# Attention and gated FFN in one kernel: another tile for unread products, a margin in the planner, new ranks

## The chip, the cores and the metric

The kernel runs on one core of one Trainium2 chip. The core has a matrix engine (TensorE, PE in the profile; its weight loads are listed as PEld), VectorE (DVE), ScalarE (ACT), GpSimd (POOL), the queue engine SyncE (SP), and 16 DMA engines. Each engine works through its own list of instructions in order. The metric is the time of one execution on the device in microseconds (us), lower is better.

## The reference

Eight batches, eight heads, 576 tokens, head size 64, and 16 extra "beacon" keys and values in front that every query sees. Causal attention over 592 keys, then a gated FFN over all 4608 tokens (512 to 1536 to 512):

```
scores = scale * q @ [beacon_k, k].T          # per batch and head
scores = where(causal, -1e9, scores)
a      = exp(scores - max) / (sum + 1e-9)
x      = a @ [beacon_v, v]                    # heads side by side: 4608 x 512
out    = (relu(x @ w_gate) * (x @ w_val)) @ w_out
```

Inputs and output are float32.

## The kernel before, in words

**Tiling.** All products are bfloat16 with float32 sums in PSUM, which has eight banks of 128 x 512. Heads go in pairs `p` (four per batch `b`). For a batch the keys and queries are loaded by `load_pair` into staging tiles `st`, cast to bfloat16 (`rounded`, tile `h`, line 487), turned by a product with the identity `ident` (`turned`, line 498), and copied out of PSUM into `kT` and, for queries, into a block-diagonal tile `diag` that holds both heads of a pair (lines 439 and 441 are the helper `copy`). `load_rest` does the same for the first tokens with the beacon keys ("F" in the order strings) and for the last ones ("L"). `load_v` loads and casts values (line 443).

**Attention.** A batch's queries are cut into blocks named A, B, C, D, E, with 128 of diag's rows for two heads at a time, and a last block F of 16 tokens that takes all heads together. `tile_step` issues the score products (line 670; 662 and 665 for E and F), the row minimum with the mask on VectorE (lines 682 and 685), the exponential on ScalarE (696), the reciprocal of the sums on VectorE (708, 703 adds two sums) and the normalization on GpSimd (715). In batch 0 the normalized blocks are turned by TensorE (line 750); in later batches by a DMA transpose on SP's queue (line 761). Then come the value products (771; 800 for F), and copies into `xT`.

**FFN.** `hidden` (lines 838, 842, 846) makes the gate and value products for 512 tokens of a batch, in the first three batches cut at token 240, with relu on ScalarE and the product on VectorE into `hT`. `project` (858) multiplies by `wo_r` in three parts of four products, copies and stores (870). The last 64 tokens of each batch are gathered for four batches at a time. The first part of the FFN of batch 0 needs the AB blocks of all four pairs and the first weights.

**The order.** Nothing is scheduled by hand. Each step is a `Task` with an engine, a cost, dependencies, buffers and a rank; `Plan.order` (line 162) simulates the engines with these costs and writes the tasks out in the order in which it starts them. Among tasks that could start at the same time the lower rank goes first. Every engine's list is fixed by this. The constants at the top (RANK, AHEAD, STEPS, ORDER0 and so on) are ranks and thresholds of that planner. STEPS gives the ranks of the groups of blocks for batches 0 to 2, WHOLE for the later ones. W_FROM and W_STEP give the earliest planned issue of the nine weight loads, which GpSimd issues (line 456) between its other work; loads of batch 1 and on wait for the first of them (`gated`).

**Unread products.** Where the planner sees TensorE idle in the first 100 us, it inserts `Filler`s: products of 256 columns (`fill`, line 917) into a bank that nobody reads. Before, they read `ident` and `mask`, two tiles that GpSimd writes (lines 379 to 387). Up to 6 us they are counted at 0.97 of the gap and a spacing of 0.2137 us, rounded down, later at 0.75 of the gap and 0.107 us.

## Time and profile before

| | us |
|---|---|
| median of 3 runs | 413.88 |
| lowest and highest | 412.75, 414.21 |
| the profiled execution's own time | 413.18 |
| its span, first to last instruction | 411.4 |
| TensorE busy | 396.4 |
| VectorE, ScalarE, GpSimd busy | 320.4, 287.0, 233.7 |

A row of the timeline reads: start, duration, engine, line, operation, output<-input, shape, count, and in brackets the idle time of the engine before it and what ended it. A row of a table of stretches reads: stretch, its length, busy time and count of PE, PEld, DVE, ACT and POOL, clock, DMA share, GB/s. A row of waits reads: who waited for whom, total, times, longest. Matmuls are pipelined: the duration of one includes its way through the array, so the spacing of the starts tells the pace.

### The profile page before, as it was taken

The numbers are of one execution on the slowest core, as the hardware profiler recorded it, in microseconds if no ns is written. First come the engines' busy times: TensorE is split into PE (matmuls) and PEld (weight loads), VectorE is DVE, ScalarE is ACT, GpSimd is POOL, SyncE is SP. The second block draws the span as 40 slices with busy tenths as digits, with TensorE's granted clock in tenths as the row PEclk, the third lists the DMA queues.
The fourth block names the chain that finished last, engine by engine and source line by source line (L and its number), as shares of the span: only waits on it lengthen the run. The fifth ranks groups of instructions, "written<-read, shape, count | busy, mean of one in ns | idle before, by whom it ended". The sixth has DMA issues, their size and how long they took to land.

```text
span 411.4 us, 10350 instructions
## 1 busy us (share of the span) xinstructions
PE 396.4 (96%) x3278; PEld 249.2 (61%) x3315; DVE 320.4 (78%) x1163; ACT 287.0 (70%) x956; POOL 233.7 (57%) x433
## 2 busy tenths in 40 slices
PE   7899999999999999999999989999999999999994
PEld 4667878487856877545558654554555545444483
DVE  6899989898989889889789898997895844233251
ACT  5898999786979899797669787874884853033040
POOL 5799769657695688568748874982761620000000
PEclk9999999999999999999999999999999999999999
DMA  8899969999999999998989699969809872110112
GB/s 199 163 236 225 211 158 174 185 186 249 177 200 184 221 229 207 200 244 151 216 216 248 192 216 170 242 153 221 158 2 209 152 105 57 57 47 0 53 53 52
DMA packets 172616, 68.03 MB, mean 165 GB/s; under 512 B 146832, under 2 KB 168080, under 8 KB 172560
## 3 DMA queue, kind: packets, MB, share of 16 engines
q1 hardware_dynamic: 167808, 62.64, 74.1%
q0 software_dynamic: 4752, 4.72, 7.0%
q8 instruction: 26, 0.43, 0.4%
q14 instruction: 30, 0.25, 0.2%
HBM read 38.27 MB, written 9.44 MB: 116 GB/s over the span
## 4 chain that ended last, share of the span: by engine, by line
PE 60%; DVE 3%; issue 2%; POOL 1%; ACT 1%; DMA 1%; SPq 0%; POOLq 0%; ACTq 0%; DVEq 0%
PE f L838 32%; PE f L858 17%; PE f L670 4%; PE f L771 4%; PE f L498 2%; PE f L662 1%; DMA st<-in_beacon_v_dram 1%; ACT pb L696 1%; POOL pb L715 1%; DVE f L685 1%; PE f L800 1%; DVE diag L441 1%; DVE osb L441 0%; DVE small L703 0%; POOL h L487 0%
## 5 line engine op out<-in xcount | busy, mean ns | idle before, releaser
L715 POOL TENSOR_SCALAR pb<-pb,small 128x576 bf16<-128x576 bf16 (+8 forms) x224 | 122.3, 564 | 76.1 <-DVE small L708 63.8
L696 ACT ACTIVATE pb<-f,small 128x64 bf16<-128x64 f32 (+6 forms) x256 | 131.6, 528 | 17.8 <-DVE small L685 9.5
L685 DVE CUSTOM_DVE_ANT_0 f<-f,mask 128x448 f32<-128x448 f32 (+7 forms) x256 | 111.7, 474 | 6.5 <-PE f L670 5.0
L842 ACT ACTIVATE g<-f 128x512 f32<-128x512 f32 (+3 forms) x156 | 71.4, 471 | 64.5 <-PE f L838 57.4
L838 PE MATMUL f<-xT,wv_r 128*128 128x512 bf16 (+3 forms) x617 | 110.6, 313 | 0.8 <-ACT pb L696 0.4
L838 PE MATMUL f<-xT,wg_r 128*128 128x512 bf16 (+3 forms) x615 | 109.4, 312 | 0.5
L846 DVE TENSOR_TENSOR hT<-g,f 128x512 bf16<-128x512 f32 (+3 forms) x156 | 79.8, 519 | 32.0 <-PE f L838 29.2
L858 PE MATMUL f<-wo_r,hT 128*128 128x512 bf16 (+1 forms) x426 | 100.7, 373 | 0.9
L838 PEld LDWEIGHTS <-wv_r 128*128 128x128 bf16 x624 | 59.0, 98 | 33.7 <-issue 0.8
L838 PEld LDWEIGHTS <-wg_r 128*128 128x128 bf16 x624 | 59.8, 98 | 31.8
L858 PEld LDWEIGHTS <-hT 128*128 128x128 bf16 x444 | 41.6, 98 | 40.4 <-issue 0.2
L696 ACT ACTIVATION_READ_ACCUMULATOR pb<-f,small 128x1 f32 x256 | 55.0, 215 | 0.0
L670 PE MATMUL f<-kT,diag 128*128 128x128 bf16 (+4 forms) x255 | 46.0, 286 | 0.8 <-DVE hT L846 0.7
L685 DVE DVE_READ_ACCUMULATOR2_ANT small<- 128x1 f32 x296 | 40.8, 138 | 0.2
L487 POOL TENSOR_SCALAR h<-st 128x512 bf16<-128x512 f32 x62 | 38.0, 620 | 4.7 <-DMA st<-in_q_dram 2.7
L441 DVE COPY osb<-f 128x512 f32<-128x512 f32 (+1 forms) x27 | 18.3, 680 | 24.0 <-PE f L858 23.7
L441 DVE CAST diag<-f 64x512 bf16<-64x512 f32 (+2 forms) x52 | 28.5, 553 | 5.0 <-PE f L498 2.7
L498 PE MATMUL f<-ident,h 128*128 128x128 bf16 (+2 forms) x320 | 29.3, 220 | 3.2 <-POOL h L487 1.5
L498 PEld LDWEIGHTS <-h 128*128 128x128 bf16 (+2 forms) x320 | 21.5, 99 | 15.1 <-POOL h L487 4.4
L715 POOL TENSOR_SCALAR xT<-xT,small 128x64 bf16<-128x64 bf16 (+4 forms) x64 | 27.4, 444 | 5.0 <-DVE small L708 4.5
L682 DVE TENSOR_REDUCE small<-f 128x1 f32<-128x512 f32 x40 | 27.3, 682 | 3.0 <-PE f L662 2.2
L696 ACT ACTIVATE xT<-f,small 128x64 bf16<-128x64 f32 (+3 forms) x64 | 27.6, 446 | 2.4 <-DVE small L685 1.7
(68 smaller groups left out, 371.9 us busy)
## 6 DMA issues: line engine op xcount, KB each, us to landing
st<-in_k_dram SPq DMA_DIRECT2D x32, 256.0 KB, 4.4
st<-in_q_dram SPq DMA_DIRECT2D x32, 256.0 KB, 4.1
out_dram<-osb SPq DMA_DIRECT2D x32, 256.0 KB, 2.8
st<-in_v_dram SPq DMA_DIRECT2D x24, 256.0 KB, 5.1
st<-in_v_dram SPq DMA_DIRECT2D x8, 224.0 KB, 4.6
wg_r<-in_moe_w_gate_dram POOLq DMA_DIRECT2D x3, 512.0 KB, 7.9
wv_r<-in_moe_w_val_dram POOLq DMA_DIRECT2D x3, 512.0 KB, 10.1
wo_r<-in_moe_w_out_dram POOLq DMA_DIRECT2D x3, 512.0 KB, 14.3
```

What stands on the lines that cost most here:

```text
L441: nc.vector.tensor_copy(dst, src)
L487: (nc.gpsimd if x.engine == "POOL" else nc.vector).tensor_scalar(to, of, by, 1.0, ALU.mult, ALU.mult)
L498: nc.tensor.matmul(to, h16.tile[:rows, a * P:(a + 1) * P], ident[:rows, :rows], start=True, stop=True)
L670: nc.tensor.matmul(view(i), t.diag.tile[:, p, j * P:j * P + P], kT[:, p, :n], start=True, stop=True)
L682: nc.vector.tensor_reduce(out=to, in_=view(i), axis=AX.X, op=ALU.min)
L685: nc.vector.tensor_tensor_reduce(out=view(i), in0=view(i), in1=msk, scale=1.0, scalar=small["t"][:, 0:1] if name in "EF" else 3.0e38, op0= ...
L696: nc.scalar.activation(ph.tile.rearrange("p a n -> p (a n)")[:, a:a + n], view(i), AF.Exp, bias=small["t"][:, low:low + 1], scale=-1.0, ac ...
L715: (nc.gpsimd if x.engine == "POOL" else nc.vector).tensor_scalar(one, one, small["t"][:, 8 + i:9 + i], 1.0, ALU.mult, ALU.mult)
L838: nc.tensor.matmul(to, w_r[:, ki, nf * P:(nf + 1) * P], x, start=(ki == 0), stop=(ki == KM - 1))
L842: r = add("ACT", c_act(w), lambda _, psg=psg, g=g: nc.scalar.activation(g.tile[:, :w], psg.tile[:, :w], AF.Relu), (a,), (psg, g), -1000 + ...
L846: hid.append(add("DVE", c_dve(w), lambda _, psv=psv, g=g, nf=nf: nc.vector.tensor_mul(hT[nf].tile[:, c0:c0 + w], g.tile[:, :w], psv.tile[: ...
L858: nc.tensor.matmul(ps.tile[:, :w], hT[nf].tile[:, t0:t0 + P], wo_r[:, nf, n0:n0 + w], start=(nf == 0), stop=(nf == NF - 1))
```

## The change

Four things are changed.

1. The unread products read a tile `ones` of 128 x 256, which VectorE writes as its first instruction. In both the stationary and the moving operand they read that tile.
2. Up to 8 us after the planned start (FILL_COLD) the number of unread products is rounded up to cover the whole gap plus 0.1 us, at a spacing of 0.2137 us before 6 us and 0.107 us after, and the task behind them is planned after their end. Later gaps are filled to 0.75 as before. Filling starts at 0.95 us of the plan instead of 1.55.
3. After 60 us of the plan, a result counts as ready later: by 0.3 us where the consumer is TensorE, by 0.15 us otherwise.
4. All ranks and thresholds of the planner are new, and small odd terms are added to the ranks so that no two are equal. The planned weight loads start at 14.78 us and follow every 3.21 us (before 15.63 and 2.53). Score tiles of later batches may hold five banks instead of four; the casts of batch 0 may go to GpSimd and VectorE but no longer to ScalarE; the holding times of batches 0 and 1 are zero.

The tasks and the work they do are the same, apart from the number of unread products: 94 before, 105 after. The lists of all engines come out in another order nearly everywhere.

```diff
-RANK = (-7.1, -27.26, -24.83, -20.12)
-AHEAD = (-15.22, 1.47, 8.0, 7.48)
+RANK = (5.77, -35.14, -19.21, -11.2)
+AHEAD = (-40.0, -1.65, 7.35, -7.54)
-W_FROM = 15.63
-W_STEP = 2.53
+W_FROM = 14.78
+W_STEP = 3.21
-FILL0 = 0.97
-FILL_FROM = 1.55
+FILL_COLD = 8.0
+FILL_PAD = 0.1
+FILL_FROM = 0.95
+SLACK_FROM = 60.0
+SLACK = (0.3, 0.15)
-LAZY = 29.32
-LAZY1 = 11.61
+LAZY = 21.01
+LAZY1 = 4.61
-SC_MOST = 4
+SC_MOST = 5
-ORDER0 = "k1 q0 q1 F k0 v2 v0 v1 q3 q2 k2 k3 v4 L v3"
+ORDER0 = "q1 k1 q0 F k0 v1 v2 v0 q3 q2 k2 k3 v4 L v3"
-CASTS = ('POOL', 'DVE', 'ACT')
+CASTS = ('POOL', 'DVE')
...
-HOLD = {0: (0.0, 18.37, 0.0), 1: (41.75, 0.0, 0.0)}
-PACE = 32.26
+HOLD = {0: (0.0, 0.0, 0.0), 1: (0.0, 0.0, 0.0)}
+PACE = 35.68
...
                 since = max(free[e], FILL_FROM)
-                n = int((at - since) * FILL / 0.107) if at > WARM else int((at - since) * FILL0 / 0.2137)
+                rate = 0.2137 if since < WARM else 0.107
+                n = int((at - since) * FILL / 0.107) if at > FILL_COLD else math.ceil((at + FILL_PAD - since) / rate) if at > since else 0
                 tile = self.filler if at < FILL_BANK else next((x[2] for x in reversed(self.banks.free) if x[0] <= since), None)
                 if n > 0 and tile is not None:
                     done.append(Filler(n, tile, self.fill))
                     part = 0
+                    if at <= FILL_COLD:
+                        at = max(at, since + n * rate)
...
-                u.ready = max(u.ready, end + (LAGS[e] if t.lag is None else t.lag))
+                u.ready = max(u.ready, end + (LAGS[e] if t.lag is None else t.lag)
+                              + (0.0 if end <= SLACK_FROM else SLACK[0] if "PE" in u.engines else SLACK[1]))
...
+    def make_ones(_):
+        nc.vector.memset(ones, 1.0)
...
+    add("DVE", 0.1, make_ones, prio=-102)
...
-            nc.tensor.matmul(to[:, :256], ident, mask.bitcast(BF16)[:, :256], start=True, stop=True)
+            nc.tensor.matmul(to[:, :256], ones[:, :P], ones, start=True, stop=True)
```

STEPS, WHOLE, F_RANK and the order strings of the later batches change likewise.

24 lines of the change are left out of this document (13 added, 11 removed).

## The prediction

> **What bounds the kernel now.** I read the busy times first, then a table of stretches, then TensorE's waits, then the order of events in the first 31 us. The first fence is from the page, the second the table of stretches: length, busy time with instruction counts, clock, DMA.
>
> ```profile
> span 411.4 us, 10350 instructions
> PE 396.4 (96%) x3278; PEld 249.2 (61%) x3315; DVE 320.4 (78%) x1163; ACT 287.0 (70%) x956; POOL 233.7 (57%) x433
> ```
>
> ```profile
> 0.00:15.00 15.00, 12.54 (x87) 8.91 (x89) 10.04 (x60) 8.74 (x18) 8.27 (x22) 1.00 0.99 224
> 15.00:31.00 16.00, 14.36 (x159) 10.33 (x157) 15.35 (x64) 15.80 (x58) 15.24 (x29) 1.00 0.96 176
> 31.00:45.00 14.00, 13.16 (x181) 10.60 (x180) 13.51 (x47) 12.09 (x40) 12.98 (x21) 1.00 1.20 227
> 45.00:235.00 190.00, 187.94 (x1724) 129.31 (x1740) 170.43 (x658) 160.28 (x569) 137.30 (x253) 1.00 1.01 202
> 235.00:257.00 22.00, 20.86 (x149) 11.05 (x149) 20.32 (x71) 17.34 (x55) 13.33 (x25) 1.00 0.96 191
> 257.00:345.00 88.00, 86.95 (x618) 44.99 (x629) 68.04 (x232) 59.15 (x192) 46.59 (x86) 1.00 0.78 152
> 345.00:400.00 55.00, 54.79 (x335) 30.12 (x338) 20.85 (x36) 12.82 (x27) 0.00 (x0) 1.00 0.11 39
> 400.00:411.40 11.40, 5.82 (x42) 3.86 (x40) 1.85 (x4) 0.76 (x2) 0.00 (x0) 0.96 0.22 48
> ```
>
> TensorE is the bound from 45 us on: its idle time from 45 to 400 is 2.06 + 1.14 + 1.05 + 0.21 = 4.5 us. All that a better order can still take there is these 4.5 us. From 15 to 31 us the other three engines are each at 95 to 99%: this is the softmax of batch 0, and the 14.36 us of TensorE are largely products that nobody reads. The last 5.6 us are the last eviction and store, whose instructions the changed order leaves as they are.
>
> **The head, event by event.** The order of TensorE's, GpSimd's and VectorE's instructions (start, duration, engine, line):
>
> ```profile
> 1.89 2.51 PE L917 MATMUL f<-mask,ident 128*128 128x256 bf16 x11 [1.89 <-POOL mask L384]
> 6.71 0.60 PE L498 MATMUL f<-ident,h 128*128 128x128 bf16 x4 [0.52 <-POOL h L487]
> 7.10 1.70 PE L917 MATMUL f<-mask,ident 128*128 128x256 bf16 x7
> 8.74 0.39 PE L498 MATMUL f<-ident,h 64*128 64x64 bf16 x4
> 10.96 1.22 PE L670 MATMUL f<-kT,diag 128*128 128x448 bf16 x9
> 12.01 1.15 PE L917 MATMUL f<-mask,ident 128*128 128x256 bf16 x9
> 12.99 0.57 PE L670 MATMUL f<-kT,diag 128*128 128x448 bf16 x2
> 30.69 0.98 PE L838 MATMUL f<-xT,wg_r 128*128 128x240 bf16 x8
> ```
>
> ```profile
> 6.03 0.62 POOL L487 TENSOR_SCALAR h<-st 128x512 bf16<-128x512 f32 x1 [0.72 <-DMA st<-in_q_dram]
> 6.86 0.69 POOL L487 TENSOR_SCALAR h<-st,scales 64x512 bf16<-64x512 f32 x1 [0.21 <-DMA st<-in_beacon_k_dram]
> 12.01 1.37 POOL L487 TENSOR_SCALAR h<-st 128x512 bf16<-128x512 f32 x2 [0.23 <-PE f L670]
> 15.23 1.32 POOL L715 TENSOR_SCALAR xT<-xT,small 128x64 bf16<-128x64 bf16 x3 [1.85 <-DVE small L708]
> 17.54 0.94 POOL L456 DMA_DIRECT2D wg_r<-in_moe_w_gate_dram  x1
> 21.14 1.86 POOL L715 TENSOR_SCALAR xT<-xT,small 128x64 bf16<-128x64 bf16 x5 [0.33 <-DVE small L685]
> 27.14 0.87 POOL L715 TENSOR_SCALAR xT<-xT,small 128x192 bf16<-128x192 bf16 x2
> 28.80 1.09 POOL L715 TENSOR_SCALAR xT<-xT,small 128x320 bf16<-128x320 bf16 x2
> 0.86 0.06 DVE L422 MEMSET scales<- 128x2 f32 x1 [0.86 <-PEq L935]
> 9.41 0.72 DVE L441 CAST diag<-f 64x192 bf16<-64x192 f32 x2 [0.67 <-ACT kT L439]
> 11.44 0.63 DVE L685 CUSTOM_DVE_ANT_0 f<-f,mask 128x448 f32<-128x448 f32 x1 [1.31 <-PE f L670]
> ```
>
> The clock column of the table reads 1.00 from the start, but the durations do not: 7 unread products of 256 columns fill the 1.64 us from 7.10 to 8.74 (0.23 each), 9 fill the 0.98 us from 12.01 to 12.99 (0.109 each). TensorE runs at half speed until about 11 us: the first scores have 2,240 columns by the program and take 1.05 us to the next row, 0.2 us at the slow spacing and the rest at the fast one, so the clock opened near 11.2. The stretch from 1.89 us to the hole before 6.71, 4.3 us long, did not open it; the next, from 6.71 on, did after 4.5 us.
>
> **The change, part by part.**
>
> *Ones, written first.* The fill's first product no longer waits for ident and mask on GpSimd but for one memset, the first on VectorE. VectorE starts at 0.86, a memset of 256 columns lies between the 0.06 us of the row and a few tenths; I take 0.1. The first product starts near 1.1 us instead of 1.89. Everything behind it on VectorE moves 0.1 us later, and the first cast of a loaded tile (a first operand of TensorE) with it: +0.1, bounds 0 and 0.3.
>
> *Fill without holes.* 105 unread products instead of 94. The third group of turns waits for a cast that GpSimd ends at 6.03 + 0.62 = 6.65 us after its load, and the changed order has one product in front of that group, as before. So the hole at 6.2 to 6.7 stays; what changes is that 5.1 us of unbroken work (1.1 to 6.2) precede it instead of 4.3. Between the third group and the first scores stand 10 + 3 + 4 = 17 products instead of 14. At full clock they are no hindrance: 6.71 + 0.22 (four turns, 512 columns) + 10 x 0.109 puts F's turns at 8.0 instead of 8.74 (F's cast ends at 7.55), its evictions end 1.4 us later as now (10.13 - 8.74), and the scores start at 9.4 instead of 10.96. At half clock three more products of 0.23 make it 11.6.
>
> By the Trainium skill, "TensorE: Matmul & The Clock Gate", section on the HAM clock gate, activity is watched in a free-running window of about 3.4 us, and the moment of the switch varies from run to run. The trace agrees with it, since 4.3 us failed and 4.5 us sufficed. By that rule alone 5.1 us would hold a whole window about every second time.
>
> I take the open clock, by the nearest row: 5.1 us is longer than the 4.5 us that sufficed.
>
> *New ranks on GpSimd.* Now the first normalization starts at 15.23, 4.3 us after the scores. In the changed order it is that of block C, whose two maxima stand third and fourth on VectorE, its reciprocal behind four more: about 3.2 us after the scores, so 12.7 (where the second cast of the row at 12.01 would still be in its way) with the open clock, 14.7 without. Then come the pair (1.09) and two casts (2 x 0.62), then the issue of the first weights (0.94): it ends at 15.9 or 18.0, against 17.54 + 0.94 = 18.48. Behind it, up to the last AB normalization of batch 0, GpSimd now takes 28.01 - 18.48 = 9.5 us; the changed order puts four more AB normalizations (0.37 each by the row of five), a C pair (1.09), two casts (1.24) and one more weight issue (0.8) in between: 9.5 + 4.6 = 14.1 us. The last AB normalization ends at 30.0 or 32.1. The first FFN product follows as now 30.69 - 28.01 = 2.7 us later: 32.7 or 34.8.
>
> In front of it stand 9.2 us of read products before and 11.4 us after, counted in columns off the program at the spacing of the full clock. Time lost there: 30.69 - 9.2 = 21.5 us before; 32.7 - 11.4 = 21.3 or 34.8 - 11.4 = 23.4 after. After that, FFN work fills gaps: the 0.84 us idle between 31 and 45 should go. So the head is worth -0.2 - 0.8 = -1.0 us with the open clock and +1.9 - 0.8 = +1.1 without. Bounds -2 and +1.9; I take -1.0.
>
> Late next is wo_r. Its three issues move on GpSimd's queue behind six more norms and five casts:
>
> ```profile
> wo_r<-in_moe_w_out_dram POOLq DMA_DIRECT2D x3, 512.0 KB, 14.3
> ```
>
> The third would be issued near 41 us instead of 38 and land near 55; it is first read by a third part of a projection, about 57 us. Cost 0, up to 1.5 if the clock stays closed. The loads of batch 1 wait on SP for the first weights; those land 2.5 us earlier or 0.5, which takes nothing away.
>
> *Casts without ScalarE, five score banks, HOLD, PACE, LAZY.* ScalarE did no cast of batch 0 before, so this does nothing by itself; two casts move from VectorE to GpSimd and are counted above. The others act only through the order.
>
> *Margin after 60 us.* It adds no instruction and no wait; the planner only believes operands to be later, by 0.3 for TensorE. What it can take is TensorE's waits:
>
> ```profile
> PE f L498 <- POOL h L487: 0.7, 2, 0.4
> PE f L838 <- ACT pb L696: 0.4, 1, 0.4
> PE f L771 <- DVE diag L441: 0.3, 1, 0.3
> PE f L498 <- ACT diag L439: 0.2, 1, 0.2
> PE f L750 <- DVE diag L441: 0.2, 1, 0.2
> PE f L498 <- DVE diag L441: 0.2, 1, 0.2
> ```
>
> From 45 to 400 us they are 2.0 us, none above 0.4, the size of the margin. I take -2.0; bounds -4.5 (all idle time) and +2.0 (as many new ones, since every order is new).
>
> *A price of the new ranks: block F.* Its scores pass VectorE, ScalarE, GpSimd and an SP transpose before its value product. The read work that TensorE has between the two, by the program, batches 0 to 7: before 7.5, 12.7, 12.3, 14.0, 15.4, 19.0, 21.9, 18.6 us; after 8.4, 13.4, 15.3, 12.5, 14.0, 13.5, 13.9, 11.9. The cover shrinks in batches 3 to 7. The shortest run with a transpose now:
>
> ```profile
> 114.34 0.44 PE L665 MATMUL f<-kT,diag 128*32 128x512 bf16 x8
> 122.78 1.20 SPq L761 DMA_TRANSPOSE pTf<-pf  x1
> 127.95 0.66 PE L800 MATMUL f<-pTf,v 128*128 128x32 bf16 x20
> pTf<-pf SPq DMA_TRANSPOSE x7, 2.9
> ```
>
> It took 13.6 us, but the transpose landed at 122.78 + 1.20 + 2.9 = 126.9, so 12.5 would have done. At 12.5 only batch 7 is short, by 0.6: +0.6; bounds 0 and 3.1 (the shortages at 13.6: 0.2 + 1.1 + 0.1 + 1.7).
>
> *Sum*, against the profiled execution's own 413.18 us: 413.2 + 0.1 - 1.0 - 2.0 + 0.6 = 410.9. The median of the three runs shown is 413.88, their span 412.75 to 414.21, so the profiled one lies inside; I add nothing.
>
> **Rivals.**
>
> *The clock stays at half until after the scores.* For it: the hole at 6.2 remains, and 4.3 us failed. Against it: the 5.1 us. The head turns from -1.0 to +1.1: 413.0, no change.
>
> *Best case.* The first FFN product comes a microsecond sooner than worked out (head -2) and all 4.5 us go: 413.2 + 0.1 - 2 - 4.5 = 406.8. Against it: a part of the idle time stands beside no late operand.
>
> *Block F decides, slower.* The transposes stand in SP's order behind longer ones of other blocks; on SP a transpose waits for those. Where the way takes a microsecond more than in the quoted run, 14.6, the shortages are 1.2 + 2.1 + 0.6 + 1.1 + 0.7 + 2.7 = 8.4 us, and the time 410.9 - 0.6 + 8.4 = 418.7. It decides from about 14.3 us on, where the shortages pass 6 us. Against it: none of TensorE's waits quoted above names this transpose, so the quoted run may merely show that nobody was in a hurry.
>
> *The fill does not do what it says* is the first rival: the hole stays by the order itself, and only its effect on the clock is open.
>
> **How the numbers follow.** A change of under 0.5% (2.1 us) is about what a measurement of this kernel can tell from none. Forecast 0.40, closed clock 0.28, block F 0.20, best case 0.12. About 0.05 of the forecast's share falls short of 0.5%. Faster 0.47, same 0.33, slower 0.20. The range runs from 407.0 to 417.0: it leaves out the lowest of the best case and the upper half of block F.
>
> **What would show it.** Right: unread products from about 1.1 us; nine or more of them at about 0.11 us each before the scores, these at 9.4; the first weights issued near 15; the first FFN product near 32.7; idle time of TensorE from 45 to 400 at 2 to 3 us; no wait of the F values over a microsecond. Wrong: products of 0.23 us after 8 us, scores after 11, a first FFN product after 34; or waits of the F values in batches 3 to 7.

## The result: slower by 0.4%

| | before | changed |
|---|---|---|
| median, us | 413.06 (20 runs) | 414.9 (20 runs) |
| lowest to highest | 411.71 to 414.26 | 412.95 to 416.59 |
| profiled execution: own time, span | 413.18, 411.4 | 415.29, 413.3 |
| ratio | 1 | 1.0040, 95% interval 1.0025 to 1.0055 |

The forecast was 410.9, faster. The changed kernel is slower by 1.0 to 2.3 us. A per cent is 4.1 us here; where ratios of several kernels are compared below, each is against runs of the kernel before on the same chip.

### The profile page after: what moved, and what is told of

The parts are those of the page before. It is cut to its first block, busy times and chain, and to the rows that moved or that the text cites. A ratio compares the mean times of both kernels' runs of the same rounds, so it can differ in the third digit from the quotient of the medians.

```text
span 413.3 us, 10385 instructions
## 1 busy us (share of the span) xinstructions
PE 396.2 (96%) x3292; PEld 248.0 (60%) x3326; DVE 323.0 (78%) x1160; ACT 288.8 (70%) x958; POOL 233.4 (56%) x435
## 4 chain that ended last, share of the span: by engine, by line
PE 79%; DMA 6%; DVE 5%; POOL 4%; issue 2%; ACT 1%; SPq 1%; DVEq 0%; POOLq 0%; ACTq 0%
PE f L851 40%; PE f L871 22%; DMA st<-in_v_dram 6%; PE f L683 6%; PE f L784 5%; PE f L511 3%; POOL xT L728 2%; DVE f L698 2%; PE f L675 1%; POOL h L500 1%; PE f L813 1%; DVE small L695 1%; PE f L678 1%; ACT pb L709 1%; SPq L534 1%
## 5 line engine op out<-in xcount | busy, mean ns | idle before, releaser
L728 POOL TENSOR_SCALAR pb<-pb,small 128x448 bf16<-128x448 bf16 (+8 forms) x224 | 121.7, 557 | 59.7 <-DVE small L721 48.9
L709 ACT ACTIVATE pb<-f,small 128x64 bf16<-128x64 f32 (+7 forms) x256 | 131.5, 530 | 10.7 <-DVE small L698 5.0
L698 DVE CUSTOM_DVE_ANT_0 f<-f,mask 128x128 f32<-128x128 f32 (+7 forms) x256 | 111.9, 473 | 4.8 <-PE f L683 3.9
L683 PE MATMUL f<-kT,diag 128*128 128x128 bf16 (+7 forms) x256 | 46.3, 286 | 0.0
L454 DVE COPY osb<-f 128x512 f32<-128x512 f32 (+1 forms) x24 | 16.3, 678 | 24.6 <-PE f L871 24.2
L511 PE MATMUL f<-ident,h 128*128 128x128 bf16 (+2 forms) x320 | 28.2, 216 | 4.4 <-POOL h L500 3.9
L728 POOL TENSOR_SCALAR xT<-xT,small 128x64 bf16<-128x64 bf16 (+2 forms) x64 | 27.0, 438 | 7.0 <-PE f L851 5.6
L709 ACT ACTIVATE xT<-f,small 128x64 bf16<-128x64 f32 (+4 forms) x64 | 27.4, 447 | 3.1 <-DVE small L698 1.6
## 6 DMA issues: line engine op xcount, KB each, us to landing
wg_r<-in_moe_w_gate_dram POOLq DMA_DIRECT2D x3, 512.0 KB, 10.4
wv_r<-in_moe_w_val_dram POOLq DMA_DIRECT2D x3, 512.0 KB, 10.1
wo_r<-in_moe_w_out_dram POOLq DMA_DIRECT2D x3, 512.0 KB, 10.4
```

What stands on the lines that cost most here:

```text
L454: nc.vector.tensor_copy(dst, src)
L511: nc.tensor.matmul(to, h16.tile[:rows, a * P:(a + 1) * P], ident[:rows, :rows], start=True, stop=True)
L683: nc.tensor.matmul(view(i), t.diag.tile[:, p, j * P:j * P + P], kT[:, p, :n], start=True, stop=True)
L698: nc.vector.tensor_tensor_reduce(out=view(i), in0=view(i), in1=msk, scale=1.0, scalar=small["t"][:, 0:1] if name in "EF" else 3.0e38, op0= ...
L709: nc.scalar.activation(ph.tile.rearrange("p a n -> p (a n)")[:, a:a + n], view(i), AF.Exp, bias=small["t"][:, low:low + 1], scale=-1.0, ac ...
L728: (nc.gpsimd if x.engine == "POOL" else nc.vector).tensor_scalar(one, one, small["t"][:, 8 + i:9 + i], 1.0, ALU.mult, ALU.mult)
```

## The profile after

The first two lines of the page, and the table of the same stretches as before (stretch, length, busy time and count of PE, PEld, DVE, ACT, POOL, clock, DMA share, GB/s):

```profile
span 413.3 us, 10385 instructions
PE 396.2 (96%) x3292; PEld 248.0 (60%) x3326; DVE 323.0 (78%) x1160; ACT 288.8 (70%) x958; POOL 233.4 (56%) x435
```

```profile
0.00:15.00 15.00, 11.21 (x94) 8.03 (x95) 10.92 (x63) 9.42 (x23) 8.59 (x23) 1.00 0.98 213
15.00:31.00 16.00, 14.87 (x164) 10.37 (x164) 15.62 (x65) 15.39 (x54) 15.37 (x31) 1.00 1.07 195
31.00:45.00 14.00, 13.75 (x192) 11.26 (x191) 13.33 (x44) 12.73 (x42) 13.37 (x21) 1.00 1.22 217
45.00:235.00 190.00, 186.54 (x1744) 128.10 (x1761) 173.27 (x655) 158.09 (x561) 135.40 (x250) 1.00 1.01 205
235.00:257.00 22.00, 21.84 (x137) 11.50 (x137) 20.65 (x80) 20.40 (x68) 16.77 (x33) 1.00 1.03 196
257.00:345.00 88.00, 86.35 (x610) 44.65 (x619) 66.58 (x222) 58.78 (x187) 43.89 (x81) 1.00 0.71 145
345.00:400.00 55.00, 54.79 (x318) 29.31 (x321) 19.79 (x33) 13.29 (x27) 0.00 (x0) 1.00 0.11 39
400.00:413.30 13.30, 6.81 (x51) 4.75 (x49) 2.80 (x6) 0.76 (x2) 0.00 (x0) 0.90 0.19 41
```

From 45 to 400 us TensorE is idle for 3.46 + 0.16 + 1.65 + 0.21 = 5.5 us, 1.0 more than before, where 2.0 less were forecast. The last stretch ends later by 1.9 us. TensorE's waits in that part, and then the head (TensorE, then GpSimd):

```profile
PE f L851 <- DVE diag L454: 1.2, 1, 1.2
PE f L511 <- POOL h L500: 1.1, 2, 0.8
PE f L851 <- DVE hT L859: 1.0, 1, 1.0
PE f L871 <- issue: 0.2, 1, 0.2
```

```profile
1.25 3.38 PE L930 MATMUL f<-ones 128*128 128x256 bf16 x15 [1.25 <-DVE scales L434]
7.25 0.40 PE L511 MATMUL f<-ident,h 128*128 128x128 bf16 x4 [1.44 <-POOL h L500]
7.49 1.25 PE L930 MATMUL f<-ones 128*128 128x256 bf16 x10
10.03 1.03 PE L683 MATMUL f<-kT,diag 128*128 128x64 bf16 x10
```

```profile
11.34 0.62 POOL L456 TENSOR_SCALAR v<-st 128x512 bf16<-128x512 f32 x1 [1.45 <-DMA st<-in_v_dram]
12.69 0.62 POOL L456 TENSOR_SCALAR v<-st 128x512 bf16<-128x512 f32 x1 [0.73 <-DMA st<-in_v_dram]
13.97 1.25 POOL L728 TENSOR_SCALAR xT<-xT,small 128x320 bf16<-128x320 bf16 x2
16.77 0.93 POOL L469 DMA_DIRECT2D wg_r<-in_moe_w_gate_dram  x1
```

The six short waits of before, none above 0.4 us, are replaced by three long ones: 1.2 us at 191.6, 0.8 at 57.0, 1.0 at 271.2. In the head the products start at 1.25 us, and ten of them pass in 1.19 us from 7.49 to 8.68, the pace of the open clock. By the spacing of the starts the clock opened near 4.5 us: products of 256 columns follow each other every 0.213 us up to 4.42 and every 0.109 us from 4.69 on. That is 3.2 us behind the first product, and ahead of the hole from 5.8 to 7.25. The scores start 0.9 us earlier than before.

To see where the span went, the program's order was laid beside the trace. The table gives the start of an instruction minus all the read TensorE work in front of it (columns at the pace of the full clock, 256 in about 0.109 us), that is, the time lost so far. It was worked out from the two traces; its last row is a duration, from the rows quoted under "The end of the kernel".

| read work in front, us | lost before | lost after | |
|---|---|---|---|
| 5 | 17.64 | 16.15 | head gain, 1.5 |
| 11.4 | 21.95 | 22.77 | given back: value loads, GpSimd |
| 30 | 24.79 | 24.81 | equal, at about 54 us |
| 32 | 24.79 | 25.78 | the wait at 57.0 us |
| 160 | 29.44 | 32.64 | the wait at 191.6 us |
| 220 | 32.42 | 33.18 | from 200 on, before loses 2.5, after 0.1 |
| 240 | 32.75 | 34.85 | the wait at 271.2 us |
| 340 | 34.54 | 35.53 | |
| last projection's start to the end | 10.9 | 11.8 | the tail |

Between 32 and 340 both lose 9.75 us. The difference of these two spans is the wait at 57 us (+1.0) and the end (+0.9). It is one profile of each kernel; how far other profiles bear it out is said below.

## The experiments

### The unread products alone

First the fills on the order of before, then the old fills on the changed order.

```diff
+    ones = cp.tile([P, 2 * P], BF16, name="ones")
...
-            nc.tensor.matmul(to[:, :256], ident, mask.bitcast(BF16)[:, :256], start=True, stop=True)
+            nc.tensor.matmul(to[:, :256], ones[:, :P], ones, start=True, stop=True)
...
+    for t, n in zip(fills, (15, 3, 1, 10, 3, 4, 10, 6)):
+        t.n = n
+    nc.vector.memset(ones, 1.0)
```

> The kernel before with every instruction in its own order, except that the unread products read a tile of ones that VectorE writes first, and that the first eight stretches of them have the changed kernel's lengths (15, 3, 1, 10, 3, 4, 10, 6 instead of 11, 2, 1, 7, 4, 3, 9, 6). Theory H (the head's gain is given back): the clock opens near 7.5 us and the first scores start 0.5 to 1.5 us earlier, but the engines behind them and the loads are full until 45 us, so the work done by 55 us and the time are the same within 0.3 us. Rival, as the prediction had it: what the scores gain stays, the time falls by 1 us (ratio 0.9975).

Measured: 412.99 us (411.62 to 417.81), ratio 0.9995 (0.9975 to 1.0015). No change, though in the profiles the scores start at 10.06 us and not at 10.96.

```diff
-        nc.vector.memset(ones, 1.0)
+        pass
...
-            nc.tensor.matmul(to[:, :256], ones[:, :P], ones, start=True, stop=True)
+            nc.tensor.matmul(to[:, :256], ident, mask.bitcast(BF16)[:, :256], start=True, stop=True)
...
+    for t, n in zip(fills, (11, 2, 1, 7, 4, 3, 9, 6)):
+        t.n = n
```

> The changed kernel, its order kept on every engine, with the unread products of the kernel before: on the identity and the mask, and in the first eight stretches with the earlier lengths (11, 2, 1, 7, 4, 3, 9, 6). The tile of ones and its initialization are gone. The clock then opens only after the scores, as it did before (unread products of 0.23 us at 8 us, scores at 10.9 or later). Theory of the prediction (the head is worth 2.1 us between open and closed clock): 416.5 to 417. Theory H (the head's gain is given back by 28 us, since loads, GpSimd, VectorE and ScalarE bound the stretch behind the scores): 414.5 to 415.3, with the first FFN product within 0.5 of 34.1.

Measured: 414.37 us, ratio 1.0041 (1.0021 to 1.0062) against the changed kernel's 1.0040. In the profile the clock stayed closed until the scores, as the timelines of TensorE and, in the last row, of GpSimd show:

```profile
7.68 1.70 PE L930 MATMUL f<-mask,ident 128*128 128x256 bf16 x7
11.22 1.24 PE L683 MATMUL f<-kT,diag 128*128 128x64 bf16 x10
16.86 0.93 POOL L469 DMA_DIRECT2D wg_r<-in_moe_w_gate_dram  x1
```

Seven products in 1.63 us (to the turns at 9.31) are half speed; the scores come 1.2 us later than in the changed kernel, and the first weights are issued 0.09 us later, since GpSimd waits for its value loads in both. The first FFN product came at 35.04 us, not within the 0.5 of 34.1 that was expected; one profile each doesn't say much there, since the loss at 30 us of work varied from 22.5 to 25.7 us between the profiles of these kernels. So the fills are worth nothing that can be measured in either order. In the profiles of the two kernels, what TensorE had gained by 10 us is lost again by 30 us of work; from 15 to 31 us VectorE, ScalarE and GpSimd are busy for 15.4 to 15.6 of 16 us.

These runs do not say what an open clock is worth, though, since the fills do not fix it. Two kernels that are described below and differ from before and after only in their last instructions show it. The first two rows are of before_first_split, with the head and the unread products of before, the third is of after_tail_before, with those of the changed kernel:

```profile
6.96 0.93 PE L917 MATMUL f<-mask,ident 128*128 128x256 bf16 x7
9.04 1.22 PE L670 MATMUL f<-kT,diag 128*128 128x448 bf16 x10
7.64 2.32 PE L930 MATMUL f<-ones 128*128 128x256 bf16 x10
```

In the first the old products run at full speed and the scores start at 9.04 us, earlier than in the changed kernel; in the second the new ones run at half speed and the scores start at 11.61. By the spacing of the starts in the profiles of all kernels of this document, the state differs from profile to profile. In the ten of the changed order with the new products the clock opened between 4.2 and 7.4 us, but in three of them it closed again near 8 us. In the nine with the old products it opened by 7.2 us in five, of which one closed again, and only between 10.7 and 14 us in four; the profile of before is one of these four.

The profiles hint that the clock does count. With the order of before, the first weights were issued at 15.8 to 16.5 us and 23.8 us were lost at 30 us of work in the three profiles in which the clock was open when the scores started (before_first_split, before_slack, before_tail_first); it was 17.5 and 18.1 us, and 24.8 and 25.6, in before and before_tail_after. In the changed order the first FFN product came at 33.4 to 34.9 us in the seven profiles with an open clock and at 35.1 to 35.6 in the three in which it had closed again. It is not the only thing: before_ones had an open clock and lost 25.2. No run changes the clock alone, so its worth stays open.

### The margin alone, and the ranks alone

```diff
-SLACK = (0.3, 0.15)
+SLACK = (0.0, 0.0)
```

> The changed kernel with SLACK = (0.0, 0.0): ranks, fills and everything else stay, only the margin goes. The order stays as it is up to 60 us and is another one behind that; the last projection's steps come out as in the kernel before. Theory S, the term of the prediction (the margin takes 2.0 us of TensorE's waits): without it the time is that of the changed kernel with the old order of its last projection (414.1) plus 2.0, so 416.1, with TensorE's idle time from 45 to 400 us back at 7 us or more. Theory N (the margin took nothing; what it did is to turn six short waits into a few long ones and to reorder the last projection): 413.6 to 414.6, and the last store group is issued before 405.5 us, as in the kernel before.

Measured: 417.59 us, ratio 1.0097 (1.0066 to 1.0128).

```diff
-                u.ready = max(u.ready, end + (LAGS[e] if t.lag is None else t.lag))
+                u.ready = max(u.ready, end + (LAGS[e] if t.lag is None else t.lag)
+                              + (0.0 if end <= SLACK_FROM else SLACK[0] if "PE" in u.engines else SLACK[1]))
```

> The kernel before with the margin alone (SLACK_FROM and SLACK, and the sum in which the planner uses them); ranks, fills and head as before. The order is the same up to 60 us; the last projection's steps come out as in the changed kernel. Theory S (the margin takes 2.0 us of waits, the tail's order costs 0.9): 413.2 - 2.0 + 0.9 = 412.1. Theory N (it takes nothing, the tail costs 0.9): 414.1, and the first of the six last stores is issued some 0.9 us later, counted from the end of the last full-width stretch, than before.

Measured: 420.1 us, ratio 1.0164 (1.0135 to 1.0194).

Both theories fall. The margin alone costs 1.6%, the ranks alone 1.0%, both together 0.4%: on the new ranks the margin saves 0.6%, on the old ones it costs 1.6%. The effects don't add, so neither has a price of its own. Each combination is another order of 3300 TensorE instructions with its own late operands. In the order of before with the margin, TensorE waits 1.8 us for a transpose and 2.0 us for VectorE in places where it waited for neither:

```profile
PE f L501 <- DVE hT L849: 2.0, 2, 1.3
PE f L774 <- DMA xT<-xT: 1.8, 1, 1.8
```

### The end of the kernel

The rows of the end, of before and then of after (TensorE's last projection, VectorE's eviction of the 512-wide group, the six last stores on SP):

```profile
400.50 5.37 PE L858 MATMUL f<-wo_r,hT 128*128 128x512 bf16 x35
404.17 0.69 DVE L441 COPY osb<-f 128x512 f32<-128x512 f32 x1 [2.97 <-PE f L858]
404.88 3.71 SPq L870 DMA_DIRECT2D out_dram<-osb  x6
```

```profile
401.49 5.37 PE L871 MATMUL f<-wo_r,hT 128*128 128x512 bf16 x35
406.03 0.69 DVE L454 COPY osb<-f 128x512 f32<-128x512 f32 x1 [3.85 <-PE f L871]
406.75 3.71 SPq L883 DMA_DIRECT2D out_dram<-osb  x6
```

The products are the same and take the same 5.37 us. But their three groups take turns differently. Before, they run four products of 512 columns, four of group A, and so on, with group B at the end; after, 512, A and B take turns, so the 512-wide group ends later and its eviction starts 4.54 us after the projection's start and not 3.67. The six stores are issued one after the other in 3.71 us in both, and the span ends 2.8 us behind the last issue. The two orders were exchanged (W, A, B are products, e evictions, d stores; m is the last gate product):

```diff
-    for t in plan.order():
+    todo = plan.order()
...
+    ORDER_OF = "W0 m A0 W1 A1 W2 A2 eW B0 eA d0 B1 d1 B2 d2 d3 eB d4 d5".split()
```

> The changed kernel, with the nine steps of the last projection and their evictions and stores put back in the order of the kernel before; all else as in the changed kernel. Theory T (the tail costs 0.9 us): in the changed kernel the first of the six last stores is issued at 406.75, 0.1 us before the last matmul ends, in the kernel before at 404.88, 1.0 us before it; the six issues follow each other on SP in 3.71 us in both, so the first of them sets the end. The time falls by 0.9 us against the changed kernel (ratio to the kernel before about 1.002), and the span ends about 5.5 us after the last matmul's end instead of 6.4. Rival: SP's issues are not the limit, the end follows the last eviction: no difference.

Measured: 414.07 us, ratio 1.0023 (1.0001 to 1.0045), 0.7 us less than the changed kernel's ratio. The two intervals overlap, so the time alone doesn't show the gain; the profile does: from the start of the last projection to the end it takes 10.9 us and not 11.8.

```diff
-    for t in plan.order():
+    todo = plan.order()
...
+    ORDER_OF = "W0 m A0 B0 W1 A1 B1 W2 A2 eW B2 eA eB d0 d1 d2 d3 d4 d5".split()
```

> The kernel before, with the last projection's steps in the order of the changed kernel; all else as before. Theory T: slower than the kernel before by 0.9 us (ratio 1.002). Rival (the end follows the last eviction): 1.000.

Measured: 414.1 us, ratio 1.0027 (1.0006 to 1.0048): the end moves to the kernel before with its price, 0.9 us in its profile (11.8 us from the last projection's start, for 10.9). The margin makes this order: it also counts for a part of a product that waits for the part before it, TensorE for TensorE, so the planner puts another group in between. In the written programs the order of after is there in before_slack and the order of before in after_slack0.

Then the end was improved: the 512-wide group first, and the stores on one queue or on two.

```diff
+    ORDER_OF = "W0 m W1 W2 eW A0 d0 d1 A1 A2 eA B0 d2 d3 B1 B2 eB d4 d5".split()
```

> The kernel before with its last projection's 512-wide products first and all six stores still on SP. With the stores on two queues as well, the ratio was 0.9971. Theory O (the order of the steps gives the gain, since it sets the first store's issue): 411.9 to 412.4. Theory I (the six issues in a row, 3.71 us, give it; an earlier first store moves the chain by no more than the eviction, 1 us or so, and SP's queue then waits for the last eviction instead): the gain with one queue is half or less, 412.6 to 413.4.

Measured: 412.9 us, ratio 0.9977 (0.9955 to 0.9998).

```diff
-... lambda _, osb=osb, r0=r0, n=n, at=at, n0=n0: nc.sync.dma_start(
+... lambda x, osb=osb, r0=r0, n=n, at=at, n0=n0: (nc.scalar if x.part else nc.sync).dma_start(
...
+    ORDER_OF = "W0 m W1 W2 eW A0 d0 d1 A1 A2 eA B0 d2 d3 B1 B2 eB d4 d5".split()
...
+    for t in stores[1::2]:
+        t.part = 1
```

> The kernel before with two edits at its end: the twelve 512-wide products of the last projection first and then the 24 of 256, so that the group with two stores is evicted first; and of the six last stores the second, fourth and sixth are issued on ScalarE's queue and not on SP's. Theory E (the end is the first store's issue plus six issues in a row on SP, 3.71 us, plus a transfer of about 2.8 us): with the first issue near 404.0 and the last one released by the last eviction near 406.9, the span ends near 409.7 to 410.2 and the time falls by 1.2 to 1.8, to 411.4 to 412.0. Theory T (the end is the transfers of the last bytes, which share the DMA engines, wherever they are issued): within 0.4 of the kernel before.

Measured: 412.1 us, ratio 0.9971 (0.9953 to 0.9990). By time, how the gain divides stays inside the intervals. By the profiles each edit gives about half: from the start of the last projection to the end it takes 10.9 us before, 10.0 with the new order and 9.2 with two queues as well. The same end on the changed kernel:

> The changed kernel with the end of the last projection in the new way: 512-wide products first, the six stores issued in turn on SP and on ScalarE's queue. The rest is untouched. If the end costs 0.85 by its order and two queues take another 1.3, the time is 414.9 - 0.85 - 1.3 = 412.7, within 0.5 of the kernel before; if the middle of the changed kernel holds back what the end gives, 414 or more.

Measured: 411.75 us, ratio 0.9960 (0.9940 to 0.9980), 3.3 us less than the changed kernel, where 2.2 was expected. In its profile the last projection starts at 400.29 us and the span ends 9.2 us later instead of 11.8:

```profile
400.29 5.37 PE L871 MATMUL f<-wo_r,hT 128*128 128x512 bf16 x36
403.80 2.82 SPq L883 DMA_DIRECT2D out_dram<-osb  x3
404.86 1.79 ACTq L883 DMA_DIRECT2D out_dram<-osb  x2
```

That is 2.6 us from the end alone. In this profile the wait at 191.6 us did not come either; below it is seen what it hangs on.

### The wait at 57 us

GpSimd waits for a value load of batch 1; the cast that TensorE needs stands behind it. SP had held the loads of batch 1 back until a staging tile was free:

```profile
52.11 0.62 POOL L456 TENSOR_SCALAR v<-st 128x512 bf16<-128x512 f32 x1 [3.06 <-DMA st<-in_v_dram]
56.38 0.61 POOL L500 TENSOR_SCALAR h<-st 128x512 bf16<-128x512 f32 x1
```

```profile
SPq L534 <- POOL h L500: 14.4, 2, 11.3
SPq L534 <- DMA wg_r<-in_moe_w_gate_dram: 8.7, 1, 8.7
```

The first theory was that the late weights `wo_r` crowd these loads, so their three issues went 3, 6 and 7 places ahead on GpSimd:

```diff
...
+    wo = [t for t in pool if t.move][6:]
+    for t, back in zip(wo, (3, 6, 7)):
+        to = pool[pool.index(t) - back]
+        todo.remove(t)
+        todo.insert(todo.index(to), t)
```

> The changed kernel with the three issues of wo_r moved 3, 6 and 7 places forward on GpSimd's list, so that they come about 2 to 4 us earlier (near 34.4, 36.5 and 38.6 us, nearer to the kernel before); all other lists as in the changed kernel. Theory W (late weights crowd the loads of batch 1): the value loads issued at 39 to 41 us land earlier than 52, GpSimd's wait of 3.06 us for them shrinks, TensorE's wait of 0.8 us at 57 for a cast queued behind them goes, and the time falls by 0.9 us. Rival: the loads are late by their own place on SP's queue; the wait at 57 stays and the time is the same.

Measured: 416.02 us, ratio 1.0078 (1.0052 to 1.0105). It costs 1.6 us: behind the earlier issues GpSimd's first cast of batch 1 starts at 39.44 us and not at 37.98, TensorE waits 0.96 us for it, these casts free the staging tiles, and the value load is still waited for (2.89 us). Next, the needed cast went ahead of the value cast:

```diff
...
+    first = [t for t in pool if t.run.__name__ == "<lambda>"][4]
+    late = next(t for t in pool[pool.index(first):] if t.run.__name__ == "shrink")
+    todo.remove(late)
+    todo.insert(todo.index(first), late)
```

> The changed kernel with one cast moved on GpSimd's list: the cast that TensorE waits for at 57 us goes ahead of the first value cast of batch 1 whose load is late (3.06 us of waiting at 49.05). No other engine's list changes. Theory C (the cast was late because it stood behind a cast that waited for its load): the wait of TensorE on this cast (0.8 us) goes, and the time falls by 0.7 to 0.9, to 414.0 to 414.2. Theory L (the load of its own staging tile is late too, since all loads of batch 1 were issued late): the wait stays, the time stays at 414.9. Theory G (it goes, but work that depends on the value cast is late next): 414.5 to 415.2 with a new wait of TensorE between 52 and 65 us.

Measured: 419.85 us, ratio 1.0149 (1.0125 to 1.0174). None of the three theories allowed as much. Its own load was later still, and all GpSimd work stood behind it:

```profile
55.68 0.62 POOL L500 TENSOR_SCALAR h<-st 128x512 bf16<-128x512 f32 x1 [7.48 <-DMA st<-in_q_dram]
63.68 0.45 PE L511 MATMUL f<-ident,h 80*128 80x80 bf16 x4 [3.70 <-POOL h L500]
```

Then load and cast moved together:

```diff
...
+    todo.remove(q_load)
+    todo.remove(v_loads[0])
+    at = todo.index(free) + 1
+    todo[at:at] = [q_load, v_loads[0]]
+    todo.remove(q_cast)
+    todo.insert(todo.index(v_cast), q_cast)
```

> The changed kernel with one load and its cast moved together: on SP's list the query load whose cast TensorE waits for at 57 us goes two places ahead, before the two value loads, as soon as its staging tile is free; on GpSimd's list its cast goes ahead of the first late value cast. Nothing else moves. The cast alone made it 419.9, its load landing at 55.7. Theory Q (the order of the loads behind the hold decides): the load lands before 51, the cast runs near 50, TensorE's wait at 57 goes, and the time falls by 0.7 to 0.9 to 414.0 to 414.2. Theory V (the value cast is needed as much): the time stays within 0.4 of 414.9, with a wait of 0.5 us or more at another place between 52 and 65 us.

Measured: 416.49 us, ratio 1.0068 (1.0045 to 1.0091). The cast now ran at 49.52, as theory Q had it, but the value load came later, and TensorE waited 1.78 us at 61.99 for a cast behind it:

```profile
54.55 0.62 POOL L456 TENSOR_SCALAR v<-st 128x512 bf16<-128x512 f32 x1 [4.42 <-DMA st<-in_v_dram]
```

None of the three orders helped. So the hold itself was taken away: three more staging tiles, with all orders kept (`Wider` hands out ten tiles in turn while the planner goes on counting seven).

```diff
-    stage_s = Slots(many(N_ST, [P, DM], FP32, "st"))
+    stage_s = Wider(many(N_ST + 3, [P, DM], FP32, "st"))
```

> The changed kernel with the same order on every engine and three more staging tiles (the planner still counts seven; the tiles are handed out in turn from ten). SP's wait of 11.3 us for a staging tile of batch 1 (27 to 38.6 us) should go for the first three loads behind it: one query and two value loads are issued near 27 us and not near 38.6 to 41. Theory ST (the wait of 0.8 us at 57 us stands at the end of that hold: GpSimd waits 3.06 us for a value load, and the cast that TensorE needs stands behind it): GpSimd's wait goes, TensorE's wait at 57 goes, the time falls by 0.8 or more, to 413.5 to 414.1. Theory BW (the DMA engines are full from 20 to 60 us, so what comes earlier pushes the weights later): the loads of the FFN weights take over a microsecond longer from issue to landing than their 10.1 to 10.4, TensorE waits for them or for what stands behind, and the time is 414.9 or more.

Measured: 413.81 us, ratio 1.0002 (0.9978 to 1.0025). One query load is issued at 27.14 us, the value loads from 27.89, and GpSimd no longer waits for them:

```profile
27.14 0.39 SPq L550 DMA_DIRECT2D st<-in_q_dram  x1
27.89 8.38 SPq L633 DMA_DIRECT2D st<-in_v_dram  x2
```

```profile
PE f L699 <- DVE kT L470: 0.4, 1, 0.4
PE f L699 <- DVE hT L875: 0.3, 1, 0.3
```

Theory ST holds: the wait at 57 us is gone, and the kernel gains 1.6 us by the ratios. That is more than the wait; in this profile the other two long waits did not come either, so its gain is not this wait alone. Theory BW falls: only `wo_r` took over a microsecond longer from issue to landing (11.6 us for 10.4; `wv_r` 10.8 for 10.1), and nothing waited for them. The same edit on the kernel before:

> The kernel before, its order kept, with three more staging tiles (ten are handed out in turn, the planner counts seven). In it SP waits 7.7 us for a staging tile of batch 1, but none of TensorE's waits stands behind it. Theory D (the hold costs only the changed order, whose loads of batch 1 come in another order and one after the other): 412.8 to 413.4, no change. Theory B (it costs both the same): 411.6 to 412.2; then the hold does not explain why the changed kernel is the slower one.

Measured: 412.2 us, ratio 0.9993 (0.9975 to 1.0010), no change. The hold costs only the changed order.

### The waits at 191.6 and 271.2 us

In front of each, an addition of one column to another on VectorE takes over ten times the 0.15 us that is the median of these additions in the kernel before. The rows of VectorE, then of GpSimd:

```profile
189.52 1.67 DVE L716 TENSOR_TENSOR small<-small 128x1 f32<-128x1 f32 x1
268.12 2.23 DVE L716 TENSOR_TENSOR small<-small 128x1 f32<-128x1 f32 x1
```

```profile
189.88 1.30 POOL L728 TENSOR_SCALAR pb<-pb,small 128x448 bf16<-128x448 bf16 x2
267.87 1.30 POOL L728 TENSOR_SCALAR pb<-pb,small 128x448 bf16<-128x448 bf16 x2
269.15 1.20 POOL L500 TENSOR_SCALAR h<-st 128x512 bf16<-128x512 f32 x2
```

The first addition starts while a cast of GpSimd's runs (189.29 to 189.90) and ends at 191.19 and GpSimd's pair at 191.18; the second ends at 270.35 and GpSimd's row of four at 270.35. Of the ten additions over 0.5 us in this profile, nine end within 0.02 us of the end of a row of GpSimd instructions without a gap. By the Trainium skill, "SBUF — State Buffer", section "Who interferes with whom", a VectorE instruction with two operands in SBUF contends with a GpSimd instruction that reads SBUF, and the later one blocks until the other has finished. The trace agrees, and shows more: an addition can stand still for several GpSimd instructions in a row, here two to four, up to 2.2 us. It does not always wait for the end of the row: in the kernel before, two of the seven additions over 0.5 us (from 120.40 and 277.82) end with a GpSimd instruction behind which the next follows without a gap. What decides that was not tried. The groups by line, of before and then of after (busy time, mean in ns):

```profile
L703 DVE TENSOR_TENSOR small<-small 128x1 f32<-128x1 f32 x40 | 11.8, 295 | 1.5 <-ACT pf L696 1.3 <-ACT pb L696 0.2
```

```profile
L716 DVE TENSOR_TENSOR small<-small 128x1 f32<-128x1 f32 x40 | 19.6, 489 | 3.1 <-ACT pb L709 1.8 <-ACT pf L709 1.1
```

The changed order has 7.8 us more of it. Whether an addition meets such a row depends on a few tenths of a microsecond: in the profile of after_first_split the one at 189.57 took 0.41 us, and the wait at 191.6 was missing. Of the eight profiles of this order with the old additions (after_slack0, whose order is another, left out) four have that wait; the one at 271.2 is in seven. The addition was written with one tensor operand:

```diff
-            sums = [add("DVE", 0.14, lambda _: nc.vector.tensor_tensor(
-                out=small["t"][:, 4:5], in0=small["t"][:, 4:5], in1=small["t"][:, 5:6], op=ALU.add), sums, (), prio, 0.18)]
+            sums = [add("DVE", 0.14, lambda _: nc.vector.tensor_scalar(
+                small["t"][:, 4:5], small["t"][:, 4:5], small["t"][:, 5:6], 1.0, ALU.add, ALU.mult), sums, (), prio, 0.18)]
```

> The changed kernel with the 40 additions of two sums (line 716) written as a tensor-scalar operation: one tensor operand, the other column as a scalar for each partition. The order of every engine's list stays. Theory P (the addition with two operands from SBUF stands still as long as GpSimd runs instructions without a gap): the 40 take 40 x 0.15 = 6 us in all and not 19.6, none over 0.5; TensorE's waits at 191.6 (1.2 us) and at 271.2 (1.0) go, and the time falls by 1.5 to 2.2, to 412.7 to 413.4. Theory O (the waits come from the order, the addition waits for an operand): durations and waits stay, 414.9.

Measured: 412.03 us, ratio 0.9968 (0.9955 to 0.9982).

```profile
L716 DVE TENSOR_SCALAR small<-small 128x1 f32<-128x1 f32 x40 | 8.3, 208 | 3.4 <-ACT pb L709 1.8 <-ACT pf L709 1.4
```

```profile
PE f L511 <- POOL h L500: 0.9, 2, 0.6
PE f L871 <- issue: 0.2, 1, 0.2
```

Theory P holds: no addition is above 0.22 us, both long waits behind VectorE are gone, that at 57 us stays. The gain, 3.0 us by the ratios, is more than the two waits (2.2 us in the profile of after).

> The kernel before with the same other form of its 40 additions (11.8 us in all, of which 17 that start inside a row of GpSimd's work take 8.3). Theory P: they take 6 us; none of TensorE's six short waits stood behind one of them, so the time falls by 0 to 0.5. Theory O: nothing moves. The two differ here only in the durations; the time tells whether the kernel before loses less by this than the changed one.

Measured: 410.35 us, ratio 0.9922 (0.9903 to 0.9942). This was a miss: the kernel before gains as much, 3.2 us, though none of its waits named an addition. So this stall, which makes two of the three long waits, does not make the changed kernel the slower one. In its profile the stretch from 32 to 340 us of read work loses 7.5 us and not 9.75: 1.3 less by 120 us and 1.0 less between 240 and 260, in places where TensorE's waits are put down to other things.

### The edits together

Both kernels with more staging tiles, the addition with one operand and the new end:

> The changed kernel with three edits: three more staging tiles, the additions as tensor-scalar, and at the end the 512-wide products first with the six stores in turn on SP and ScalarE's queue. If the gains add (1.1 to 1.5 for the staging, 1.0 for the wait that only the additions take away, 2.2 to 3.1 for the end): 414.9 - 4.3 to 414.9 - 5.6, so 409.3 to 410.6. If two of them take away the same wait: 411 to 411.8.

Measured: 407.57 us, ratio 0.9858 (0.9842 to 0.9875), below the forecast 409.3 to 410.6: a miss to the good side.

> The kernel before with the same three edits. If the changed order is worth something once its waits are gone (its margin and its ranks): 411.5 to 412.1, over 1 us above the changed kernel with these edits. If the two orders are worth the same: within 0.5 of it.

Measured: 408.5 us, ratio 0.9887 (0.9869 to 0.9904). The changed kernel with these edits is the fastest of all that ran, 1.2 us below the other by the ratios; the intervals just overlap. The forecast for before_best, 411.5 to 412.1 or near the other kernel, had no term for the 3.2 us that the additions are worth there; its first value was too high by 3 us, and only the sign of the difference fits the first theory.

## Why the prediction was wrong

**Ones written first, +0.1.** Near enough: the memset took 0.27 us and not 0.1, VectorE's next instruction began at 1.14 us and not at 0.86, inside the bound of 0.3, and the fill started at 1.25 us for a forecast 1.1. Nothing behind it shows a cost.

**The clock.** Taken as open, and in this profile it was, but the reason given does not hold: it took 4.3 us of work as too little and 4.5 as enough, and here 3.2 us opened it. That the forecast state came true was luck in part: in three of ten profiles the clock closed again, and the profile that the working started from was one of the four in nine in which the kernel before opened it late. The hole that the prediction left open as a danger is where these part: the clock closed again in the four profiles in which TensorE idled 1.77 to 2.06 us there, and stayed open in the seven in which it was open ahead of a hole of at most 1.76 us. The scores came at 10.03 us and not at 9.4: the hole in front of the third turns grew from 0.52 to 1.44 us, since GpSimd's cast was later, where the prediction had left the hole as it was.

**The head, -1.0: failed.** The step that fell is the issue of the first weights, which "ends at 15.9 or 18.0" and was taken at 15.9 for the open clock. With the clock open it ended at 17.70, because two value casts in front waited 1.45 and 0.73 us for their loads, and the prediction had chained GpSimd's list without these loads. From there to the first FFN product it took 16.4 us, near the 16.8 of the working, so this product came at 34.13 us, not at 32.7. Lost time at 30 us of work was equal (24.79 and 24.81), the changed kernel with an open clock and the kernel before with a closed one. That the clock would be worth 2.1 us between open and closed is not borne out: the fills alone move neither kernel's time, and the profiles hint at 1 to 2 us at this place, in either kernel.

**Loads of batch 1: "which takes nothing away" failed.** They do wait for the first weights (8.7 us), but then 11.3 us more for a staging tile that GpSimd's casts free. Behind this stands the wait at 57 us, +1.0 in the span; without the hold the ratio falls by 1.6 us. The prediction counted GpSimd's longer list for the FFN's start and not for what the list frees. Its worry about `wo_r` was at the wrong place: no wait of TensorE names it.

**The margin, -2.0: failed.** The short waits did go, all six. What was wrong is the bound for what comes in their place: between 32 and 340 us of work the loss is 9.75 us in both, because two of the long waits came (1.2 and 1.0 us; the one at 57 us lies ahead of this stretch) and, between 200 and 220, 2.4 us were saved. Both of these waits hang on the stalled addition. The bound of 4.5 us for all that could be taken was too low, too: it is TensorE's idle time by the profile, and the stretch lost 9.75 us; the other form of the addition took 3.7 us out of it in the changed kernel, where the two waits were 2.2. With the additions mended the same stretch loses 6.0 us in the changed order and 7.5 in that of before, one profile each, so the order is worth about 1.5 us where nothing stalls; that after_best is below before_best fits this. That the margin as such does it is not shown: on the old ranks it cost 1.6%, on the new ones it saved 0.6%.

**Block F, +0.6.** Not seen: no wait in the middle names the F values. The rival that rested on it fell.

**The end, counted at 0: failed.** "Whose instructions the changed order leaves as they are" is true of the instructions and false of their order: +0.9, shown by exchanging the two ends (11.8 and 10.9 us in the profiles of both kernels).

Sum on the spans: 411.4 + 0 (head) + 1.0 (wait at 57 us) + 0 (the middle) + 0.9 (the end) = 413.3, the span measured. This is the account of one profile of each kernel, and only the end is as firm as its figure. Up to 30 us of work the loss of one and the same order differs by up to 1.8 us between profiles, and in those of after_tail_before and after_first_split, in which the wait at 191.6 did not come, the way from 30 to 340 us of work loses about as much as in the kernel before. So which share of the 1.0 to 2.3 us by which the changed kernel is slower is the hold and which is the head stays open. None of the rivals was what happened in these two profiles. The closed clock's 413.0 lies nearest, for a reason that did not occur in the profile of after.

## What to carry to other kernels

Look at the last instructions of a kernel as closely as at the longest stretch: they have no cover, and a row of stores on one queue (3.71 us for six) starts only when the first of them may. When an engine's list grows, ask what its instructions free, and not only who reads their results: here a staging tile held eleven microseconds of loads. An instruction that takes ten times its usual time without any wait beside it is a wait; compare its end with the ends on the other engines. And before a term is read off the first microseconds of one profile, read a second one: here the clock opened at another time in each.

## What the runs showed of the hardware that was not expected

- A one-column addition with both operands in SBUF stood for up to 2.23 us, over up to four GpSimd instructions without a gap; with one tensor operand and a column as scalar it took at most 0.22 us, and each kernel got 3 us faster.
- The issue of one query load on SP took 0.42 us near 24 us and 3.97 us at 41.44 us in the changed kernel. Why was not tried.
- From the first of six stores issued in a row to the end of the span it takes 3.71 us of issue and 2.8 us behind it. With the new end and two queues the issues took 2.82 us, gaps for the evictions included.
- The clock of TensorE opened at another time in each profile of one and the same head: with the head of before, 256 columns took 0.109 us from about 5 us on in before_first_split and before_slack and from about 11 us on in before. An open clock closed again in the four profiles with an idle time of 1.77 to 2.06 us in front of the third turns.
- The loss of the head varied by three microseconds between profiles of kernels with nearly the same start (22.5 to 25.7 us at 30 us of read work). Single profiles can't settle a head of this kind; repeated timing settles only what the whole edit is worth.
